# Attention and gated FFN on one Trainium2 core: weight blocks in 2 KB runs, gates ahead of values, and one batch's values rounded elsewhere than on ScalarE

## Chip, cores and metric

One core of a Trainium2 chip (trn2). The metric is device time in microseconds (us) of one execution. An execution of this kernel takes some 2 us longer than the span that its profile shows.

## The reference

```python
q, k, v: [8, 8, 576, 64]            # batch, heads, sequence, head_dim, fp32
kv  = einsum('bhsd,bhse->bhde', k, v)
o   = einsum('bhsd,bhde->bhse', q, kv)
a   = o / sqrt(mean(o*o, -1) + 1e-6) * g_norm
x   = a.transpose(0, 2, 1, 3).reshape(4608, 512)
xn  = x / sqrt(mean(x*x, -1) + 1e-6) * rms_g
out = (silu(xn @ w_gate) * (xn @ w_val)) @ w_out    # w_gate, w_val: 512 x 1536; w_out: 1536 x 512
```

## The kernel before

The kernel works batch by batch: up-projections (gate and value) and down-projection of one batch on TensorE, with the attention of the next batch threaded between them. All matrix work is in bf16; everything arrives in fp32, is staged in one of seven buffers, and is rounded into its bf16 place by VectorE, ScalarE or GpSimd. The rounding of gate and value weights also multiplies the rows by the norm's scale. The order on each engine is written by hand. Batch 0 is the start-up: its first half runs while the first weights come in, and the remaining weights come in during its second half.

Gate and value weights are 1536 columns wide and come in five column blocks; the first four are 256 columns wide, which is 1 KB of fp32 per row, 512 KB per block:

```python
W_BLOCKS = [(0, 2), (2, 4), (4, 6), (6, 8), (8, 12)]      # in units of 128 columns
def load_w(blk, name, queue):
    ...
    queue.dma_start(out=ap, in_={"g": wg_view, "v": wv_view}[name][:, :, j0 * 128 : j1 * 128])
# ...
for blk in range(2):                  # order of the transfers: g0, v0, g1, v1, then g2, v2, g3, v3, g4, v4
    for name in ("g", "v"):
        load_w(blk, name, nc.sync)
```

The first products of batch 0 come in that order too: gate 0, value 0, rows of the attention output, gate 1, two transposes, value 1. TensorE then goes on to the second half of the rows. Loads, the stores of the output and the transposing transfers that turn the queries all share the sync queue, in the order written:

```python
ffn.down_out(2)                       # down_out(1), above, issued two output stores; the next line issues two more
ffn.down_out(3)
cast_q(2, slice(4, 8), DVE)
# ...
for c in range(T):
    atts[2].q_rows(c)                 # four transposing transfers of batch 2's queries
# ... in the loop over batches, n == 1 (the up-projection of batch 1):
steps[0] += [lambda i=i: cast_kv(2, "v", i, SC) for i in (0, 1)]     # batch 2's values, on ScalarE
steps[1] += [lambda i=i: cast_kv(2, "v", i, SC) for i in (2, 3)]
steps[0] += [lambda name=name: cast_kv(2, name, NS, GP) for name in ("k", "v")]
```

ScalarE also does the silu of each gate product, in the order written: a silu stands behind the casts ahead of it. A product lies in a bank of PSUM (TensorE's output memory), which TensorE writes again only when the silu has read it.

## Time and profile before

| | us |
|---|---|
| median of the first three runs | 321.17 (320.72 to 321.30) |
| the run that the profile shows | 322.3, span 320.4 |
| before first gate product | 17.39 |
| first gate product to batch 1's up-projection | 39.10 |
| batch 1's first gate product to batch 2's key-value products | 7.83 |
| from there to the next gate product | 3.16 |
| from there to the last matmul | 248.83 |

In the lines PE is TensorE (PEld its weight loads), ACT ScalarE, DVE VectorE, POOL GpSimd and SPq the sync queue. A timeline line is: start, duration, engine, source line, operation, output and inputs, shapes, the number of instructions put together, and in brackets the idle time ahead of it with what ended it. Neither the duration nor the bracket is to be trusted for a stall: matmuls overlap, so the step from one start to the next is what counts.

### The profile page before, as it was taken

What the parts mean: (1) busy time and instruction counts of PE and PEld (TensorE: products, weight loads), DVE (VectorE), ACT (ScalarE), POOL (GpSimd) and SP (SyncE); (2) the same over time, 40 slices, a digit from 0 to 9 for tenths busy, and PEclk for the clock granted to TensorE, in tenths of its full rate; (3) what the DMA queues carried; (4) which work ended last, traced back from release to release, by engine and by line L of the source; (5) the groups of instructions that cost most, each with busy time, mean ns of one, the idle gap of its engine ahead of it and who ended that gap; (6) DMA issues with size and microseconds to landing.
All of it is one profiled execution on the core that took longest, in us unless ns stands there. A gap on an engine that the chain in (4) does not pass through costs nothing.

```text
span 320.4 us, 5591 instructions
## 1 busy us (share of the span) xinstructions
PE 309.1 (96%) x2138; PEld 151.1 (47%) x2175; DVE 181.5 (57%) x371; ACT 178.9 (56%) x318; POOL 21.0 (7%) x44
## 2 busy tenths in 40 slices
PE   7799999999999999999999999999999999999995
PEld 3475456454444444444444444444544444444443
DVE  4676857479528932794179517950696069604310
ACT  3576457675768376837673767467644374233321
POOL 1153442100000000000000000000000000000000
PEclk9999999999999999999999999999999999999998
DMA  7999999988299747943793379946002610240014
GB/s 255 348 349 387 380 374 305 232 248 211 49 150 315 179 103 190 288 110 75 198 316 103 66 183 215 319 103 190 13 0 51 172 43 1 50 149 0 1 35 98
DMA packets 74440, 54.90 MB, mean 171 GB/s; under 512 B 42281, under 2 KB 67117, under 8 KB 74413
## 3 DMA queue, kind: packets, MB, share of 16 engines
q1 hardware_dynamic: 74044, 53.89, 60.7%
q10 hardware_dynamic: 368, 0.66, 0.6%
q8 instruction: 17, 0.28, 0.3%
q14 instruction: 11, 0.08, 0.1%
HBM read 37.75 MB, written 9.44 MB: 147 GB/s over the span
## 4 chain that ended last, share of the span: by engine, by line
PE 78%; DMA 14%; DVE 2%; SPq 2%; issue 1%; another core or an unknown queue 1%; ACT 1%; POOL 0%; ACTq 0%; DVEq 0%
PE g_ps L490 26%; PE v_ps L490 25%; PE o_ps L532 22%; DMA st<-in_moe_w_out_dram 7%; DMA st<-in_moe_w_val_dram 3%; DMA st<-in_v_dram 2%; PE att_ps L275 1%; DMA st<-in_k_dram 1%; SPq L194 1%; DMA xnt<-xna 1%; DVE xna L394 1%; DMA out_dram<-o_sb 1%; PE att_ps L354 1%; SPq L401 1%
## 5 line engine op out<-in xcount | busy, mean ns | idle before, releaser
L496 DVE TENSOR_TENSOR h_sb<-silu,v_ps 128x512 bf16<-128x512 bf16 x104 | 71.0, 684 | 100.1 <-ACT silu L495 72.4
L490 PE MATMUL v_ps<-xnt,wv_sb 128*128 128x512 bf16 x409 | 106.1, 379 | 0.6
L490 PE MATMUL g_ps<-xnt,wg_sb 128*128 128x512 bf16 x398 | 104.6, 379 | 1.6 <-ACT silu L495 0.7
L495 ACT ACTIVATE silu<-g_ps 128x512 bf16<-128x512 f32 x104 | 61.9, 596 | 67.9 <-PE g_ps L490 52.7
L532 PE MATMUL o_ps<-wo_sb,h_sb 128*128 128x512 bf16 x386 | 87.1, 379 | 0.5
L490 PEld LDWEIGHTS <-wv_sb 128*128 128x128 bf16 x416 | 40.6, 98 | 49.2 <-DVE wv_sb L204 0.5
L532 PEld LDWEIGHTS <-h_sb 128*128 128x128 bf16 x420 | 40.7, 98 | 47.9 <-issue 0.3
L490 PEld LDWEIGHTS <-wg_sb 128*128 128x128 bf16 x416 | 39.5, 98 | 47.7 <-issue 1.6
L106 ACT COPY o_sb<-o_ps 128x512 f32<-128x512 f32 (+1 forms) x34 | 19.7, 581 | 38.0 <-PE o_ps L532 35.3
L106 ACT CAST vb<-st 128x512 bf16<-128x512 f32 (+2 forms) x34 | 19.5, 626 | 6.9 <-DMA st<-in_v_dram 6.9
L394 DVE TENSOR_TENSOR xna<-outa,s1y 128x512 bf16<-128x512 bf16 x28 | 17.9, 685 | 0.0
L377 DVE TENSOR_REDUCE ssq<-sqt 128x16 f32<-128x1024 bf16 x14 | 17.1, 1220 | 0.5
L377 DVE TENSOR_REDUCE ssq<-sq 128x16 f32<-128x1024 bf16 x14 | 17.1, 1220 | 0.5
L106 ACT CAST qb<-st 128x1024 bf16<-128x1024 f32 (+1 forms) x17 | 15.4, 943 | 2.4 <-DMA st<-in_q_dram 2.2
L106 ACT CAST kb<-st 128x512 bf16<-128x512 f32 (+1 forms) x25 | 14.0, 619 | 0.0
L363 ACT ACTIVATE sq<-att_ps 128x512 bf16<-128x512 f32 x14 | 7.6, 594 | 4.3 <-PE att_ps L354 3.6
L376 DVE TENSOR_TENSOR sq<-sq,gsq 128x512 bf16<-128x512 bf16 x14 | 5.9, 422 | 4.9 <-ACT sq L363 4.9
L633 PE MATMUL att_ps<-kv_all 128*128 128x512 bf16 (+1 forms) x21 | 7.3, 471 | 1.2 <-DVE sel L622 1.2
L108 POOL CAST wo_sb<-st 128x512 bf16<-128x512 f32 x12 | 7.5, 657 | 7.3 <-DMA st<-in_moe_w_out_dram 7.3
L363 ACT ACTIVATE sqt<-o_ps 128x512 bf16<-128x512 f32 x14 | 7.6, 597 | 0.0
L368 ACT CAST outa<-att_ps 128x512 bf16<-128x512 f32 x14 | 7.5, 592 | 0.0
L368 ACT CAST outa<-o_ps 128x512 bf16<-128x512 f32 x14 | 7.5, 592 | 0.0
(145 smaller groups left out, 179.8 us busy)
## 6 DMA issues: line engine op xcount, KB each, us to landing
out_dram<-o_sb SPq DMA_DIRECT2D x14, 512.0 KB, 3.0
st<-in_q_dram SPq DMA_DIRECT2D x6, 1024.0 KB, 7.2
st<-in_k_dram SPq DMA_DIRECT2D x6, 1024.0 KB, 10.3
st<-in_v_dram SPq DMA_DIRECT2D x6, 1024.0 KB, 11.2
st<-in_moe_w_out_dram SPq DMA_DIRECT2D x6, 512.0 KB, 11.5
st<-in_moe_w_gate_dram SPq DMA_DIRECT2D x4, 512.0 KB, 10.0
st<-in_moe_w_val_dram SPq DMA_DIRECT2D x4, 512.0 KB, 10.4
st<-in_k_dram SPq DMA_DIRECT2D x4, 288.0 KB, 4.8
```

What stands on the lines that cost most here:

```text
L106: engine.copy(out=dst, in_=src)
L108: engine.tensor_copy(out=dst, in_=src)
L363: SC.activation(out=self.sq[i][:, :, 0, g:H:2, :], in_=self.banks[i][g], func=ACT.Square)
L368: SC.copy(out=rows[:, :, g:H:2, :], in_=self.banks[i][g])
L376: DVE.tensor_tensor(out=sq[:, 1], in0=sq[:, 0], in1=gsq8, op=OP.mult)
L377: DVE.reduce_sum(out=self.ssq[:, c], in_=sq, axis=AX.X)
L394: DVE.tensor_tensor(out=self.xna[c], in0=self.outa[c], in1=self.alpha[:, c, :].to_broadcast([128, H, D]), op=OP.mult)
L490: PE.matmul(ps, lhsT=wt[:, s, j * 128 : (j + 1) * 128], rhs=x[:, s, :], start=(s == 0), stop=(s == NS - 1),)
L495: SC.activation(out=silu, in_=g_ps, func=ACT.Silu)
L496: DVE.tensor_tensor(out=self.h[:, j, :], in0=silu, in1=v_ps, op=OP.mult)
L532: PE.matmul(self.o_ps[c], lhsT=self.h[:, j, c * 128 : (c + 1) * 128], rhs=wo_sb[:, j, :], start=(j == 0), stop=(j == NF - 1),)
L633: PE.matmul(ps[:, 0:w], lhsT=warm_sb[:, 0:128], rhs=warm_sb[:, 0:w], start=True, stop=True, skip_group_check=True)
```

## The change

Its intent: weight blocks two to a buffer in 2 KB runs (the first two gate blocks stay in 1 KB runs), so that transfers go faster; the two first gate blocks ahead of the value blocks, so that TensorE does not wait for gate 1; the value blocks by halves of the rows; the two small vectors issued from ScalarE's queue; and batch 2's values off ScalarE, so that silu does not stand behind a load.

```diff
-    def load_w(blk, name, queue):
-        j0, j1 = W_BLOCKS[blk]
...
+    def load_w(name, blks, split):
...
+            if split:
+                w_st[name, b] = whole[:, :, at : at + w]
+            else:
+                w_st[name, b] = flat[:, NS * at : NS * (at + w)].rearrange("p (s f) -> p s f", s=NS)
+                nc.sync.dma_start(out=w_st[name, b], in_=view[:, :, j0 + at : j0 + at + w])
...
+        if split:
+            for s in (0, 2):
+                nc.sync.dma_start(out=whole[:, s : s + 2], in_=view[:, s : s + 2, j0 : j0 + at])
...
-    load_q0(0, nc.sync)
-    nc.sync.dma_start(out=gam[0:NS, :], in_=moe_rms_g.rearrange("(s p) -> s p", p=128))
+    nc.scalar.dma_start(out=gam[0:NS, :], in_=moe_rms_g.rearrange("(s p) -> s p", p=128))
... (the same for g_norm)
+    load_q0(0, nc.sync)
...
-    for blk in range(2):
-        for name in ("g", "v"):
-            load_w(blk, name, nc.sync)
+    load_w("g", (0, 1), False)
+    load_w("v", (0, 1), True)
...
+    for blk, s in ((0, 0), (0, 1), (1, 0), (0, 2), (1, 1), (1, 2)):
+        round_w(blk, "v", s, GP)
... (products in the order gate 0, rows, gate 1, value 0, transposes, value 1)
-    for blk in (2, 3, 4):
-        for name in ("g", "v"):
-            load_w(blk, name, nc.sync)
+    for name in ("g", "v"):
+        load_w(name, (2, 3), True)
+    for name in ("g", "v"):
+        load_w(name, (4,), False)
... (GpSimd's roundings of blocks 2 and 3: gates first)
-            steps[0] += [lambda i=i: cast_kv(2, "v", i, SC) for i in (0, 1)]
-            steps[1] += [lambda i=i: cast_kv(2, "v", i, SC) for i in (2, 3)]
-            steps[0] += [lambda name=name: cast_kv(2, name, NS, GP) for name in ("k", "v")]
+            steps[0] += [lambda: cast_kv(2, "k", NS, GP)]
+            steps[0] += [lambda i=i: cast_kv(2, "v", i, GP) for i in (0, 1, NS)]
+            steps[2] += [lambda i=i: cast_kv(2, "v", i, DVE) for i in (2, 3)]
```

## The prediction

> **What bounds the kernel now.** First the busy shares and the forty slices of the page, for the bound.
>
> ```profile
> PE 309.1 (96%) x2138; PEld 151.1 (47%) x2175; DVE 181.5 (57%) x371; ACT 178.9 (56%) x318; POOL 21.0 (7%) x44
> ...
> PE   7799999999999999999999999999999999999995
> ...
> DMA  7999999988299747943793379946002610240014
> ```
>
> TensorE is busy in every slice but the first two and the last; the transfers fill only the first eight slices (64 us). Each slice is 8 us. So the change, which touches loads and roundings of the first 65 us, can pay only where TensorE stands still in that stretch. As busy time hides gaps and overlaps, I read TensorE's timeline by start times: four 512-column matmuls advance 0.86 us (59.08 to 59.94), two groups of eight 128-column ones 0.87 us, eight 256-column ones 0.87 us (22.57 to 23.45). What advances more than that is a stall.
>
> The timeline of TensorE, 17 to 23 us, where the first weights come in:
>
> ```profile
> 18.08 0.61 PE L507 MATMUL g_ps<-xnt,wg_sb 128*128 128x128 bf16 x8
> 18.53 1.04 PE L507 MATMUL v_ps<-xnt,wv_sb 128*128 128x256 bf16 x8
> 19.40 0.61 PE L443 MATMUL o_ps<-kv_all,qt 128*128 128x128 bf16 x8
> 20.02 0.28 PE L507 MATMUL g_ps<-xnt,wg_sb 128*128 128x256 bf16 x1
> 20.48 0.94 PE L507 MATMUL g_ps<-xnt,wg_sb 128*128 128x256 bf16 x7 [0.17 <-POOL wg_sb L204]
> 21.25 0.61 PE L288 MATMUL att_ps<-identity,xna 128*128 128x128 bf16 x8
> ```
>
> Between 19.40 and 21.25 lie 0.45 + 0.87 us of work in 1.85 us: a stall of 0.5 us, waiting for the second gate block's roundings.
>
> GpSimd's timeline tells when the blocks landed, by the waits that a transfer ended:
>
> ```profile
> 19.33 1.09 POOL L204 TENSOR_SCALAR wg_sb<-st,rowscale 128x256 bf16<-128x256 f32 x2 [1.41 <-DMA st<-in_moe_w_gate_dram]
> ...
> 23.83 0.48 POOL L204 TENSOR_SCALAR wv_sb<-st,rowscale 128x256 bf16<-128x256 f32 x1 [1.02 <-DMA st<-in_moe_w_val_dram]
> ...
> 26.83 0.48 POOL L204 TENSOR_SCALAR wv_sb<-st,rowscale 128x256 bf16<-128x256 f32 x1 [1.02 <-DMA st<-in_moe_w_val_dram]
> ...
> 32.22 1.36 POOL L204 TENSOR_SCALAR wv_sb<-st,rowscale 128x512 bf16<-128x512 f32 x2 [3.97 <-DMA st<-in_moe_w_val_dram]
> ```
>
> Blocks of 512 KB in 1 KB runs: two in the 3.00 us from 23.83 to 26.83, so 1.50 us each. The two 1 MB blocks in 2 KB runs: 5.39 us to 32.22, so 2.70 us per MB against 3.00. The table of stretches says the same of the rate:
>
> ```profile
> 14.00:24.00 10.00, 9.57 (x114) 7.65 (x115) 7.46 (x22) 7.41 (x16) 5.70 (x13) 1.00 1.10 350
> 26.00:36.00 10.00, 9.84 (x48) 4.41 (x47) 6.91 (x13) 5.98 (x11) 2.78 (x5) 1.00 1.05 388
> ```
>
> The last number is GB/s: 350 with 1 KB runs, 388 with runs of 2 KB and more, with the engines full (share over 1) both times.
>
> Last, ScalarE and then TensorE at the start of batch 1's up-projection:
>
> ```profile
> 57.62 0.64 ACT L495 ACTIVATE silu<-g_ps 128x512 bf16<-128x512 f32 x1
> 60.82 1.14 ACT L106 CAST vb<-st 128x512 bf16<-128x512 f32 x2 [2.56 <-DMA st<-in_v_dram]
> 61.86 0.59 ACT L495 ACTIVATE silu<-g_ps 128x512 bf16<-128x512 f32 x1
> ```
>
> ```profile
> 60.80 1.03 PE L490 MATMUL v_ps<-xnt,wv_sb 128*128 128x512 bf16 x4
> 62.50 1.02 PE L490 MATMUL g_ps<-xnt,wg_sb 128*128 128x512 bf16 x4 [0.67 <-ACT silu L495]
> ```
>
> ScalarE's in-order stream stands 2.56 us behind batch 2's values; the second silu comes late, its PSUM bank is not free, and TensorE steps 1.70 us where 0.86 is due: 0.84 us lost. It is the largest single stall of TensorE after 17 us. A small one stands at 46.01, where four matmuls take 1.09 instead of 0.86: 0.2 us until the second down-weight block, landed at about 45.2, is rounded.
>
> **What the Trainium skill says.** "DMA: Bandwidth & Descriptors", § Why small descriptors are slow (HBM only): each packet carries about 3 cycles beside one per 32 bytes. As an estimate from that page, 1 KB runs cost 35 cycles and 2 KB 67, so two short ones are 4% dearer than a long one; this trace shows 3.00 against 2.70 us, 11%, and I use the trace. The same page, § Issuing engines are not separate DMA queues: issuing from another engine saves only sequencer time. The trace agrees: issuing the two small vectors holds the sync queue 0.55 and 0.70 us. "SBUF — State Buffer", § Who interferes with whom: a GpSimd instruction and a VectorE one that takes the shared ports block each other. That bears on moving casts to GpSimd: its 128x512 casts took 0.59 us each in the pairs of 1.18 us, 0.70 in those that met a busy VectorE (1.40 and 1.44).
>
> **The change, part by part.**
>
> *Small vectors to ScalarE's queue.* It frees 1.25 us of the sync queue (3.14 to 4.44), but the next issue, at 4.49, follows the first key block's landing (its cast starts at 4.47), and the compiled order lists a wait on that transfer there, in both kernels. So the third key block is issued no earlier, and the transfers are full by then. Worth 0 to 0.1 us; I count 0.
>
> *2 KB runs.* The first value MB and the MBs of gate and value of blocks 2 and 3 gain 0.30 us each, so all that comes later lands about 0.9 us sooner. TensorE gets only the 0.2 us at 46.01 of this. The rest lands in slack.
>
> *Gates before values, values by halves of the rows.* Order now: gate 0, gate 1, upper rows of values 0+1, lower rows. Four pieces of 512 KB as before, so the second piece lands in time for the second gate block, whose roundings end about 18.3 instead of 20.9. The 0.5 us stall goes. TensorE, starting as before at 17.39, does gate 0 and sums (to 18.53), rows (0.45), gate 1 (0.87) and is at value 0 at 19.85. But the third piece lands at 19.25 less 0.15 = 19.1, the fourth 1.35 later, 20.45. GpSimd rounds six pieces at 0.47 each: (0,0) 19.57, (0,1) 20.04, (1,0) 20.5, (0,2) 20.97, (1,1) 21.4, (1,2) 21.9, while ScalarE does (0,3) and (1,3) from 20.45, to 21.4. Value 0's third row block is there at 21.0. TensorE then needs two matmuls of the first unit and four of the second: 0.65, so 21.65; the two transposes 0.45, to 22.1; value 1 0.87, to 22.97. Before, this point was 22.57: +0.40. I chose to let the waits stand wholly on the path: the fixed order on TensorE has nothing to put there.
>
> *ScalarE's table load* slips from 21.29 to 21.4, the first silu from 22.58 to about 22.7; its bank is next needed about 24.7. Free.
>
> *Later roundings.* Blocks 2 and 3 now round gates before values on GpSimd. The value half needed at about 27.6 lands near 25.9 (20.45 + 4 x 1.35), its first two roundings end at 26.8. No new stall.
>
> *Batch 2's values.* Four ScalarE casts (1.14 + 1.12 us) become two on GpSimd, two on VectorE. The values land about 59.8 instead of 60.8; GpSimd does two casts and the tail at 0.6 to 0.7, to about 61.8; VectorE does its two in 0.75 after the third product, to about 63.4; TensorE wants them from 63.6 on. The silu no longer waits: -0.84.
>
> Sum: +0.40 - 0.20 - 0.84 = -0.64 us, which 321.17 turns into 320.5. From batch 2 on nothing differs but the start, so the shift is carried to the end.
>
> **The rivals.**
> 1. *The value wait grows.* Should the third piece land late, or GpSimd be blocked by VectorE (0.70 for 0.47 on six pieces), value 0 waits another 0.5 to 0.8 us. For it: the chain third piece, four roundings, TensorE has no slack. Time 321.0 to 321.3.
> 2. *The value wait is short.* If the roundings run nearer the landings, or the start moves up 0.2 us with the freed sync queue, the reorder costs nothing: 319.9 to 320.1. Against it: the wait on the first transfer.
> 3. *The gain at 62 us turns into another wait.* The key-value products follow 1.7 us later, and the rotated queries of batch 2 come by transposing transfers landing near 66.4, when TensorE, 0.64 us sooner, reaches them at about 66.3. Losing half of the 0.84 gives 320.9. In favour: those issues follow the output stores, which follow TensorE at 55 us, not the removed stall. Against: only the last quarter of the products needs the last transpose.
> 4. *The loads bound everything*, as the chain of waits suggests with its 14% for transfers. Then 0.9 us more would come off: 319.6. Against it: TensorE's timeline has no such waits between 27 and 60 us other than the 0.2.
>
> **Range and chances.** The measured runs of before span 0.6 us, and the rivals lie between 319.6 and 321.3. I predict 320.5, with 319.7 to 321.4 holding it 8 times in 10. Two per cent would be 6.4 us, ten times my sum; the stalls of the whole touched stretch do not add up to 2 us. So: faster 0.005, same 0.985, slower 0.01.
>
> **What would show it.** Right: in the new timeline of TensorE no step of 1.7 us near 61 us, and no gap before the second gate block, but about 1.1 us of gap within value 0 near 20 us; the stretch 26 to 62 us 0.2 us shorter; GB/s near 385 from about 19 us on; batches from the third on moved as a block by some 0.6 us. Wrong: the first values rounded by 20 us (reorder free), a wait before batch 2's products on GpSimd's casts or on a transpose (rival 3), or later batches whose period of 32.6 us (123.07 to 155.69 in the chain of waits) changes.

## The result, and the profile after

| | median us | lowest to highest | runs |
|---|---|---|---|
| before | 321.41 | 320.72 to 321.96 | 6 |
| after | 321.40 | 320.82 to 322.33 | 6 |

The ratio is 1.0002, with a 95% interval of 0.9981 to 1.0022: the same. (A ratio is the mean time of one kernel's fast runs over that of the other's of the same rounds, so not quite the ratio of the medians.) I had predicted 320.5; what was measured is 0.9 us above that, at the very edge of the range. The class was right, the gain was not there.

The page of the changed kernel. TensorE's busy time is what it was, and the transfers fill the same slices.

```profile
span 319.0 us, 5591 instructions
...
PE 308.9 (97%) x2138; PEld 151.3 (47%) x2175; DVE 181.4 (57%) x372; ACT 176.6 (55%) x313; POOL 22.8 (7%) x48
...
PE   7899999999999999999999999999999999999995
...
DMA  7999999888389757924792499946002600230014
```

This span is 1.4 us shorter than the one of before, and that is the trap: the profiled run of before took 322.3 us, that of after 321.24. The two traces differ by about 1.1 us, the two kernels by nothing.

The table of stretches (busy time of PE, PEld, DVE, ACT, POOL; granted clock, DMA share, GB/s) shows that the 2 KB runs do what they were meant to, 385 GB/s where there were 350:

```profile
14.00:24.00 10.00, 9.51 (x111) 7.74 (x110) 8.19 (x22) 7.54 (x15) 7.48 (x16) 1.00 1.05 385
26.00:36.00 10.00, 10.00 (x48) 4.51 (x46) 7.03 (x15) 6.00 (x10) 2.81 (x5) 1.00 1.05 387
```

GpSimd's timeline tells the landings. The first values had landed by 17.84; the last rows of blocks 2 and 3 (24.45) and block 4 (29.90) landed 2.3 to 2.4 us sooner than in the trace of before (26.83, 32.22):

```profile
14.66 2.74 POOL L207 TENSOR_SCALAR wg_sb<-st,rowscale 128x256 bf16<-128x256 f32 x6 [0.87 <-DMA st<-in_moe_w_gate_dram]
17.84 2.74 POOL L207 TENSOR_SCALAR wv_sb<-st,rowscale 128x256 bf16<-128x256 f32 x6 [0.44 <-DMA st<-in_moe_w_val_dram]
21.74 1.99 POOL L207 TENSOR_SCALAR wg_sb<-st,rowscale 128x256 bf16<-128x256 f32 x4 [1.15 <-DMA st<-in_moe_w_gate_dram]
24.45 1.84 POOL L207 TENSOR_SCALAR wv_sb<-st,rowscale 128x256 bf16<-128x256 f32 x4 [0.72 <-DMA st<-in_moe_w_val_dram]
29.90 1.36 POOL L207 TENSOR_SCALAR wv_sb<-st,rowscale 128x512 bf16<-128x512 f32 x2 [3.62 <-DMA st<-in_moe_w_val_dram]
```

TensorE's timeline over the first weights. Gate 1 (18.23) now follows without a gap, and value 0 waits within itself, after its second matmul: it takes 1.30 us to the transposes (19.10 to 20.40) where 0.87 is due. So the wait is 0.43 us by the steps (the bracket says 0.25), where I had expected about 1.1; my own sums gave 0.93 (19.85 to 21.65 for 0.87 of work).

```profile
18.23 1.04 PE L510 MATMUL g_ps<-xnt,wg_sb 128*128 128x256 bf16 x8
19.10 0.38 PE L510 MATMUL v_ps<-xnt,wv_sb 128*128 128x256 bf16 x2
19.73 0.83 PE L510 MATMUL v_ps<-xnt,wv_sb 128*128 128x256 bf16 x6 [0.25 <-POOL wv_sb L207]
20.40 0.61 PE L291 MATMUL att_ps<-identity,xna 128*128 128x128 bf16 x8
...
21.72 1.04 PE L510 MATMUL o_ps<-xnt,wg_sb 128*128 128x256 bf16 x8
```

Then ScalarE and TensorE at 60 us. No cast stands between the silus, and gate follows value in 0.86 us (59.94 to 60.80). But after the key-value products there is a new wait, on the transposed queries:

```profile
58.47 0.60 ACT L498 ACTIVATE silu<-g_ps 128x512 bf16<-128x512 f32 x1 [1.08 <-PE g_ps L493]
60.20 0.60 ACT L498 ACTIVATE silu<-g_ps 128x512 bf16<-128x512 f32 x1 [1.13 <-PE g_ps L493]
```

```profile
59.94 1.03 PE L493 MATMUL v_ps<-xnt,wv_sb 128*128 128x512 bf16 x4
60.80 1.03 PE L493 MATMUL g_ps<-xnt,wg_sb 128*128 128x512 bf16 x4
61.66 1.03 PE L493 MATMUL v_ps<-xnt,wv_sb 128*128 128x512 bf16 x4
62.62 0.82 PE L278 MATMUL att_ps<-vb,kb 128*64 128x64 bf16 x40
...
66.09 0.29 PE L357 MATMUL o_ps<-kv_all,qt 64*128 64x64 bf16 x8 [0.36 <-DMA qt<-qb]
66.31 0.60 PE L493 MATMUL g_ps<-xnt,wg_sb 128*128 128x512 bf16 x2
```

From the key-value products (62.62) to the next gate product (66.31) TensorE took 3.69 us; before, it had been 3.16 (64.32 to 67.48). The queue's own timeline shows why the queries are late: the four transposing issues take 6.0 us and stand behind the four output stores.

```profile
55.00 3.70 SPq L555 DMA_DIRECT2D out_dram<-o_sb  x4
58.81 6.01 SPq L319 DMA_TRANSPOSE qt<-qb  x4
```

So the profile shows the stall that I wanted away gone (7.83 to 7.00 us), 0.53 us of it spent again on another wait, and times that do not differ. What remained to be found out was whether the 0.84 us had been there to gain at all.

### The profile page after: what moved, and what is told of

Same layout as the page of the kernel before. It is cut to its first block, busy times and chain, and to the rows that moved or that the text cites. A ratio compares the mean times of both kernels' runs of the same rounds, so it can differ in the third digit from the quotient of the medians.

```text
span 319.0 us, 5591 instructions
## 1 busy us (share of the span) xinstructions
PE 308.9 (97%) x2138; PEld 151.3 (47%) x2175; DVE 181.4 (57%) x372; ACT 176.6 (55%) x313; POOL 22.8 (7%) x48
## 4 chain that ended last, share of the span: by engine, by line
PE 87%; DMA 6%; SPq 2%; issue 1%; DVE 1%; another core or an unknown queue 1%; ACT 1%; POOL 1%
PE v_ps L493 27%; PE g_ps L493 27%; PE o_ps L535 26%; DMA st<-in_moe_w_val_dram 3%; DMA st<-in_q_dram 2%; PE att_ps L278 1%; SPq L319 1%; DMA qt<-qb 1%; PE v_ps L535 1%; PE g_ps L535 1%; DMA out_dram<-o_sb 1%; POOL wv_sb L207 1%; PE o_ps L510 1%; PE att_ps L357 1%
## 5 line engine op out<-in xcount | busy, mean ns | idle before, releaser
L106 ACT CAST vb<-st 128x512 bf16<-128x512 f32 (+2 forms) x30 | 17.2, 628 | 3.3 <-DMA st<-in_v_dram 3.3
```

Source lines behind the costliest of these rows:

```text
L106: engine.copy(out=dst, in_=src)
```

## The experiments

All kernels gave correct results and ran in five timed rounds. A job of four kernels shares eleven runs of the kernel before on the same chip. The theory going in, called S: the stall at 62 us is the difference of two times (when batch 2's values land, and when TensorE wants the PSUM bank behind ScalarE's casts), so its size is a property of one run. The rivals: the gain is real and given back in the wait for the queries; the new order of the first blocks eats it; the loads bound everything.

### First job: both kernels again, and the values alone

`before_again` and `after_again` are the two kernels unchanged.

> The kernel before, unchanged, for a second trace and for the noise. Theory N (the 0.75 us by which the changed kernel reached the first gate matmul sooner, 16.64 against 17.39 us, is chance in the first loads): this trace reaches that matmul at some other time, 16.4 to 17.2, its span is 319.0 to 320.0, and the stalls (0.5 us before the second gate block, 0.84 us at 62 us) are there again. Theory V (the moved small vectors made the head start): it is at 17.3 to 17.5 again. Time ratio 1.000 within 0.0015.

> The changed kernel, unchanged. Theory N: the first gate matmul anywhere from 16.4 to 17.4 us; the time ratio to before 0.998 to 1.000, as what is gained after that matmul is about 0.4 us in its first trace (0.84 at 62 us and 0.1 before, less 0.53 at the batch 2 products). Theory V: matmul at 16.5 to 16.8 again and ratio about 0.996 (1.2 us).

| | median us | lowest to highest | ratio to before (95%) |
|---|---|---|---|
| before of this job, 11 runs | 321.42 | 320.49 to 323.37 | |
| before_again | 321.13 | 320.76 to 321.78 | 0.9993 (0.9969 to 1.0017) |
| after_again | 321.38 | 320.84 to 321.99 | 0.9995 (0.9969 to 1.0022) |

The second trace of the very same kernel is the most telling one. ScalarE and TensorE in it:

```profile
59.56 1.14 ACT L106 CAST vb<-st 128x512 bf16<-128x512 f32 x2 [1.86 <-DMA st<-in_v_dram]
60.61 0.59 ACT L495 ACTIVATE silu<-g_ps 128x512 bf16<-128x512 f32 x1
```

```profile
60.25 1.03 PE L490 MATMUL v_ps<-xnt,wv_sb 128*128 128x512 bf16 x4
61.25 1.02 PE L490 MATMUL g_ps<-xnt,wg_sb 128*128 128x512 bf16 x4
```

The casts start at 59.56 instead of 60.82, and the stall is 1.00 - 0.86 = 0.14 us instead of 0.84. The size of the "largest single stall" of my prediction belonged to one run, in which the load trailed: of the 16 signals that the trace holds for that load, 14 had come by 59.38, the last two at 60.32 and 60.80; in this trace all had come by 59.54. This gives a rule that can be checked: the casts and the silu put the next gate product 1.69 us after the start of the casts (60.82 to 62.50 in the first trace, 59.56 to 61.25 in this one), or 0.86 us after the value product ahead of it, whichever is later.

`values_only` is the kernel before with the last hunk of the diff alone; `values_undone` is the changed kernel without that hunk.

> Before, with batch 2's values rounded off ScalarE and nothing else. If that is the whole source of the gain after 22 us: no 0.84 us stall at 62 us, and 0.3 to 0.6 us of it lost again where the batch 2 products wait for the transposed queries, ratio 0.9985 to 0.9995 (0.15 to 0.5 us). Rival (the gain is kept whole when the loads are not sooner): no wait at the products, ratio 0.9974 (0.84 us).

> The changed kernel, with batch 2's values on ScalarE again. Values land near 58.5 us there, so if ScalarE's wait for the values made the stall, the second silu is held until about 59.7 rather than 61.9 and the stall at the fourth gate product is small, 0 to 0.3 us, even with the casts on ScalarE: then the sooner loads, not the move, would be enough. Rival: the stall is back with 0.5 us or more. Ratio to before 0.998 to 1.001.

| | median us | lowest to highest | ratio to before (95%) |
|---|---|---|---|
| values_only | 321.25 | 320.58 to 322.55 | 0.9999 (0.9972 to 1.0026) |
| values_undone | 321.48 | 320.61 to 322.69 | 1.0002 (0.9973 to 1.0032) |

In `values_only` the stall is gone (7.00 us to the key-value products), the wait for the queries that I had expected did not show (3.16 us to the next gate product: a miss), and the time does not move. GpSimd's first cast of the values starts at 60.27 there; by the rule, casts on ScalarE would have put the gate product at about 61.9, where TensorE did it at 61.16. So the move spared this trace an estimated 0.7 to 0.8 us, which six runs with an interval of ± 0.9 us cannot show. `values_undone` tells more. Its casts are on ScalarE as before:

```profile
58.86 1.14 ACT L106 CAST vb<-st 128x512 bf16<-128x512 f32 x2 [1.10 <-DMA st<-in_v_dram]
59.90 0.59 ACT L498 ACTIVATE silu<-g_ps 128x512 bf16<-128x512 f32 x1
```

58.86 + 1.69 is 60.55, and TensorE comes to that product at 61.17: no stall, though its first gate product (17.38) was as late as in the first trace of before (17.39). In this trace the sooner loads alone are enough to end the stall; the move of the casts then has nothing left to do. The other eight traces with the long runs of blocks 2 and 3 (`late_after`, below, aside) agree: GpSimd's first cast of the values starts between 57.89 and 59.11, and 1.69 us later is in each at least 0.2 us before TensorE did the gate product. In the traces with short runs (`late_before` and the faulty `runs_1kb`, below, aside) it is the other way: 0.11 to 0.84 us of stall in the four with casts on ScalarE, and an estimated 0.7 to 0.8 in `values_only` and in `runs_1kb_mended`, below (60.08 against 60.95).

### Second job: values made late, the order undone, the short runs

`late_before` and `late_after` add two loads of 256 KB, never read, ahead of batch 2's values, into unused ends of the staging buffers:

```diff
         for name in ("k", "v"):
             alloc_kv(b, name)
+            if b == 2 and name == "v":
+                for i in (-1, -2):
+                    load_spare(i, 3)      # 128 rows x 8 heads of batch 3's keys, in 256-byte runs
             load_kv(b, name, nc.sync)
```

> Before, with two loads of 256 KB in short runs, never read, queued ahead of batch 2's values. Theory S (ScalarE's wait for the values is the stall, and its size is only how late the values land: landing + 1.05 us of casts + 0.6 us of silu, less the time when TensorE wants the bank; 0.8 us in the first trace, 0.14 in the second, where they landed 1.3 us sooner): the values land 2.6 to 3.8 us later, near 62.1 to 63.3, and TensorE stands 2.5 to 3.8 us there; ratio 1.007 to 1.012. Rival (the stall has another cause): 0.1 to 0.8 us as before, ratio 1.000 to 1.002.

> The changed kernel with the same two loads. Theory S: the silus go on, TensorE waits only later, at batch 2's key-value products, for GpSimd's third cast (the tail), about 2 us after the landing: 1.0 to 1.8 us, ratio 1.003 to 1.005; so the move is worth 1.5 to 2 us where the values are late, and nothing where they are in time. Rival: the late landing costs both kernels the same, ratio as late_before within 0.001.

| | median us | lowest to highest | ratio to before (95%) |
|---|---|---|---|
| before of this job, 11 runs | 321.69 | 321.12 to 322.30 | |
| late_before | 322.92 | 322.42 to 324.71 | 1.0039 (1.0017 to 1.0061) |
| late_after | 321.94 | 321.11 to 322.49 | 1.0003 (0.9988 to 1.0018) |

With late values the whole change is worth 1.0039 - 1.0003, about 0.36% or 1.2 us. In `late_before` I had expected twice that; its profiled run, at 324.71 us, was its slowest, and the others left no trace. In `late_after` I had expected 1.003 to 1.005 and a wait of 1.0 to 1.8 us for GpSimd's casts, and neither came. Lines of TensorE's waits (total, times, longest), one of each kernel, late_before first:

```profile
PE g_ps L504 <- ACT silu L509: 2.3, 1, 2.3
```

```profile
PE o_ps L371 <- DMA qt<-qb: 1.0, 1, 1.0
```

In the one the silu is waited for, in the other not, and there the queries are waited for instead. So the mechanism of the prediction is shown, and so is its rival. But the 1.2 us are not the worth of the move alone, as the long runs land the values sooner in `late_after`, late as they are (ScalarE's casts in `late_before`, then GpSimd's in `late_after`):

```profile
62.09 1.14 ACT L106 CAST vb<-st 128x512 bf16<-128x512 f32 x2 [4.17 <-DMA st<-in_v_dram]
```

```profile
60.20 1.73 POOL L108 CAST vb<-st 128x512 bf16<-128x512 f32 x3 [4.23 <-DMA st<-in_v_dram]
```

By the rule, casts on ScalarE would have cost `late_after` an estimated 0.9 us (60.20 + 1.69 is 61.89, and TensorE did that product at 60.99), and its wait for the queries, 1.14 us by the steps (4.30 for 3.16), is longer than that. What the move alone is worth with late values was not run. From the up-projection's start to the key-value products `late_before` took 11.02 us, 4.0 more than 7.00, of which the wait is 2.45 by the steps (60.46 to 63.77 for 0.86; the bracket says 2.3). The rule holds here too (casts at 62.09, gate product at 63.77). The other 1.6 us are the clock (columns as in the stretches above; the last but two is the granted clock):

```profile
60.00:64.00 4.00, 1.72 (x8) 0.68 (x7) 0.25 (x1) 1.91 (x4) 0.61 (x1) 0.99 1.21 342
64.00:68.00 4.00, 4.00 (x49) 1.70 (x48) 1.78 (x3) 1.84 (x4) 0.00 (x0) 0.58 0.71 115
```

After the gap the granted clock was 0.58 in this stretch, and two groups of four matmuls stepped 1.55 and 1.85 us, where 0.86 and 0.96 are usual. The Trainium skill, "TensorE: Matmul & The Clock Gate", § Part 1: The HAM clock gate (the "warmup" mystery), tells of such a gate: half rate after an idle window of about 3.4 us. The trace agrees on the half rate (its record of the clock holds 0.5 for 3.41 us, from 63.91 on), but here an idle gap of 2.3 us came before it.

`order_undone` loads blocks 0 and 1 and orders their roundings and products as the kernel before does (1 KB runs, g0 v0 g1 v1), and leaves the other parts of the change in. `runs_1kb` was meant to undo the 2 KB runs alone:

```diff
-    load_w("v", (0, 1), True)
+    load_w("v", (0, 1), False)
...
-        load_w(name, (2, 3), True)
+        load_w(name, (2, 3), False)
```

> The changed kernel with loads, roundings and products of blocks 0 and 1 in the old order (gate 0, value 0, gate 1, value 1 in 1 KB runs), the rest as changed. My prediction's term (new order costs 0.40 us): from the first gate matmul to the second half's first product about 0.4 us less than the mean of the new order's traces (5.08, 5.49, 4.84: 5.14), so 4.7 to 4.8, ratio 0.999. Theory N (both orders wait for a load whose landing moves from run to run against the first gate matmul): anywhere from 4.8 to 5.3, as the old order gave 5.18, 5.11 and 4.97; ratio 0.999 to 1.001.

> The changed kernel with blocks 0 to 3 in 1 KB runs, block by block, gates of 0 and 1 still ahead of values. If shorter runs cost 0.30 us per MB: 1.50 us between landings instead of 1.35 up to block 3, the fifth megabyte block lands about 0.9 us later than in the changed kernel at equal start, and as all of that is slack the ratio is 0.999 to 1.001. Rival (the loads bound the stretch to 60 us): 0.6 to 0.9 us longer, ratio 1.002 to 1.003.

| | median us | lowest to highest | ratio to before (95%) |
|---|---|---|---|
| order_undone | 320.98 | 320.14 to 322.26 | 0.9979 (0.9960 to 0.9998) |
| runs_1kb | 321.99 | 321.65 to 322.52 | 1.0008 (0.9994 to 1.0022) |

`runs_1kb` was a faulty experiment. GpSimd's order of roundings was left as it is for halves of the rows, where the first row block of value 1 comes ahead of the third of value 0. With whole blocks this makes value 0 wait for the landing of value 1. GpSimd:

```profile
18.54 0.94 POOL L207 TENSOR_SCALAR wv_sb<-st,rowscale 128x256 bf16<-128x256 f32 x2 [0.68 <-DMA st<-in_moe_w_val_dram]
20.05 1.85 POOL L207 TENSOR_SCALAR wv_sb<-st,rowscale 128x256 bf16<-128x256 f32 x4 [0.57 <-DMA st<-in_moe_w_val_dram]
```

TensorE waited 1.2 us there by the bracket (1.5 by the steps). So the run tells nothing of short runs, and was mended in the last job.

### Third job: the vectors, the order again, the transposes first

`vectors_only` is the kernel before with the two small vectors issued from ScalarE's queue ahead of the first query load; `vectors_undone` is the changed kernel with them back on the sync queue, behind it. `order_undone_again` is a repeat. `turns_first` is `order_undone` with the four transposes issued ahead of the last two output stores:

```diff
     ffn.down_out(2)
-    ffn.down_out(3)
     cast_q(2, slice(4, 8), DVE)
+    att2 = Att(2)
+    for c in range(T):
+        att2.q_rows(c)
+    ffn.down_out(3)
```

> Before, with the two small vectors on ScalarE's queue and nothing else. First gate matmul so far: 17.39, 16.81, 17.12, 17.18 us with them on the sync queue; 16.64, 17.29, 17.38, 16.42, 16.15, 16.61 with them moved. Theory N (chance): 16.2 to 17.4, third key block issued at about 4.5 again, ratio 0.999 to 1.001. Theory V (the move gains about 0.4 us on average): 16.1 to 16.9, ratio 0.998 to 0.9995.

> The changed kernel with the two small vectors on the sync queue again. Theory N: first gate matmul anywhere from 16.2 to 17.4, ratio to before 0.999 to 1.001. Theory V: 16.9 to 17.4, and slower than the changed kernel by about 0.4 us, ratio 1.0005 to 1.002.

> The changed kernel with blocks 0 and 1 in the old order, once more, as its first ratio (0.9979, 0.9960 to 0.9998) is the only one clear of 1. If the old order is truly better than the new one by about 0.5 us: ratio 0.997 to 0.999 again. If it was chance: 0.999 to 1.001.

> As order_undone, and the four transposing transfers of batch 2's queries issued ahead of the second pair of output stores. They wait for the query casts alone, so they start near 56.2 us rather than 58.8 and the last lands near 63 us: no wait at batch 2's products (it was 0.25 to 0.96 us in four traces), from the key-value products to the next gate product 3.15 to 3.2 us instead of 3.3 to 4.3. Ratio 0.997 to 0.9985. Rival (the wait only moves, to the third batch's loads behind the late stores): 3.2 us there, but the gain lost later and ratio as order_undone.

| | median us | lowest to highest | ratio to before (95%) |
|---|---|---|---|
| before of this job, 11 runs | 321.20 | 320.70 to 322.32 | |
| vectors_only | 320.97 | 320.43 to 321.51 | 0.9987 (0.9971 to 1.0004) |
| vectors_undone | 321.12 | 320.89 to 321.69 | 0.9996 (0.9981 to 1.0011) |
| order_undone_again | 321.26 | 320.60 to 323.56 | 0.9999 (0.9978 to 1.0020) |
| turns_first | 320.67 | 320.36 to 321.08 | 0.9979 (0.9963 to 0.9995) |

The gain of `order_undone` was not repeated; from the first gate product to the second half its traces took 5.37 and 4.89 us, within the 4.84 to 5.49 of the new order's. One of the runs of the repeat, at 323.56 us, is the profiled one, and shows what such an outlier can be. A line of TensorE's timeline and three stretches of it:

```profile
11.31 0.69 PE L276 MATMUL att_ps<-vb,kb 64*64 64x64 bf16 x18 [1.96 <-ACT vb L106]
```

```profile
8.00:12.00 4.00, 1.96 (x30) 1.38 (x30) 1.75 (x5) 1.37 (x3) 0.00 (x0) 0.88 1.02 356
12.00:16.00 4.00, 4.00 (x44) 2.40 (x44) 1.94 (x10) 1.76 (x4) 1.36 (x3) 0.50 1.09 355
16.00:20.00 4.00, 3.73 (x32) 2.60 (x31) 2.47 (x8) 2.14 (x5) 3.37 (x8) 0.77 1.07 372
```

Batch 0's values were late, TensorE stood 1.96 us, and then ran at half clock from 11 to 18 us; its first gate product was at 19.83. The wait of 2 us made some 3 us of loss. The other slow runs left no trace, but their granted clock is on record. Of the 119 runs of the four jobs that enter the fit below, 17 have a mean clock of 0.995 or less; they took 322.37 us in the mean, the other 102 took 321.16, and all four above 322.6 us are among the 17 (323.37 of before at 0.993, 323.17 of `turns_before` at 0.994, this one at 0.989). So a spell at half clock goes with the slow end of the scatter; what began it in those runs is not known.

`vectors_only` shows the rule of 1.69 us at work once more: the casts start at 59.28, the gate product at 60.97.

### Fourth job: transposes first in both kernels, and the short runs mended

The first two add the move of the transposes alone to the changed kernel and to the kernel before; the third repeats `turns_first`; the fourth is `runs_1kb` with GpSimd's order put right, value block 0 whole ahead of block 1, and blocks 2 and 3 loaded as g2 v2 g3 v3 as before:

```diff
-    for blk, s in ((0, 0), (0, 1), (1, 0), (0, 2), (1, 1), (1, 2)):
+    for blk, s in ((0, 0), (0, 1), (0, 2), (1, 0), (1, 1), (1, 2)):
```

> The changed kernel with one thing more: the four transposing transfers of batch 2's queries are issued ahead of the last two output stores of batch 0, not behind all four. Theory (what is gained before 62 us is partly given back in the wait for these transposes): the wait, 0.36 and 0.21 us in the two traces of the changed kernel, is gone, the step from the key-value products to the next gate products is 3.16 us, and the time falls by that much, 0.2 to 0.4 us: ratio 0.9985 to 0.9995 to the kernel before. Rival (the wait costs nothing, or the loads issued behind the stores pay for it): the ratio stays at 0.9995 to 1.0005, or a wait on batch 3's loads appears near 80 us.

> The kernel before with that move of the transposes alone. Theory: its traces show no wait for the transposes above 0.1 us, as the stall for the silu or a later start comes first, so nothing is to be had: ratio 0.9995 to 1.0005, and the stall near 62 us, 0.1 to 0.9 us by the landing of batch 2's values, stands. Rival (the early transposes are worth 0.2% of themselves, which is what the kernel with the order undone seemed to say): 0.998.

> A repeat of the kernel with the order of the first blocks undone and the transposes first, which gave 0.9979 (0.9963 to 0.9995). If that was the kernel's own: 0.997 to 0.999 again and a step of 3.16 us to the next gate products. If it was chance of the job's runs, as the first 0.9979 of the order undone seems to have been: 0.999 to 1.000.

> The changed kernel with the first four weight blocks loaded block by block in runs of 1 KB, the first two gate blocks still ahead of the value blocks, and GpSimd's roundings in the order in which blocks land (the earlier kernel of this kind kept an order made for halves of the rows, so that value block 0 waited for value block 1). Theory (the longer runs land the later loads some 0.9 us sooner, but that is slack but for about 0.2 us): the wait ahead of value block 0 is again 0 to 0.7 us, from the first gate product to the second half's first product 4.8 to 5.5 us, pieces land 1.50 us apart, ratio 0.9995 to 1.001. Rival (loads bound the first 60 us): 0.9 us more, ratio 1.002 to 1.003.

| | median us | lowest to highest | ratio to before (95%) |
|---|---|---|---|
| before of this job, 11 runs | 321.54 | 320.70 to 322.52 | |
| turns_after | 321.37 | 321.01 to 321.58 | 0.9991 (0.9974 to 1.0008) |
| turns_before | 321.21 | 320.75 to 323.17 | 0.9996 (0.9970 to 1.0021) |
| turns_first_again | 320.65 | 320.05 to 321.59 | 0.9971 (0.9952 to 0.9990) |
| runs_1kb_mended | 321.08 | 320.61 to 321.81 | 0.9984 (0.9965 to 1.0002) |

In `turns_after` the wait for the queries is gone. Its sync queue and TensorE:

```profile
55.38 1.23 SPq L555 DMA_DIRECT2D out_dram<-o_sb  x2
56.93 5.63 SPq L319 DMA_TRANSPOSE qt<-qb  x4
62.67 1.19 SPq L555 DMA_DIRECT2D out_dram<-o_sb  x2
```

```profile
65.83 0.40 PE L357 MATMUL o_ps<-kv_all,qt 64*128 64x64 bf16 x16
66.16 1.04 PE L493 MATMUL g_ps<-xnt,wg_sb 128*128 128x512 bf16 x4
```

The step is 3.16 us (63.00 to 66.16), and the ratio lies where the theory put it, though its interval includes 1. `turns_before` has nothing to gain from it and gains nothing; its stall is 0.11 us, and the rule hits it again (casts at 60.03, gate product at 61.72). `runs_1kb_mended` is not slower than the changed kernel: value 0 follows gate 1 almost without a wait (0.96 us for 0.87), presumably because its third row block is GpSimd's third rounding there and not its fourth (4.94 us from the first gate product to the second half, against 5.08 and 5.49), and the later, slower blocks find slack. The repeat of `turns_first` came out as the first time, with the same median within 0.02 us: it beats the kernel before by 0.2 to 0.3%, which is still "the same" at 2%. The changed kernel was not run beside it as it is.

The stages of the traces, from TensorE's start times (us):

| trace | first gate product | to second half | to batch 1 | to key-value products | to next gate product | to last matmul | run |
|---|---|---|---|---|---|---|---|
| before | 17.39 | 5.18 | 33.92 | 7.83 | 3.16 | 248.83 | 322.30 |
| before_again | 16.81 | 5.11 | 34.01 | 7.13 | 3.28 | 248.67 | 321.03 |
| turns_before | 16.69 | 5.79 | 33.95 | 7.11 | 3.16 | 248.61 | 321.32 |
| after | 16.64 | 5.08 | 33.90 | 7.00 | 3.69 | 248.56 | 321.24 |
| after_again | 17.29 | 5.49 | 33.98 | 7.00 | 3.37 | 248.48 | 321.96 |
| turns_after | 17.00 | 5.05 | 33.95 | 7.00 | 3.16 | 248.48 | 321.06 |
| turns_first | 16.37 | 4.94 | 34.16 | 7.00 | 3.16 | 248.62 | 320.36 |
| turns_first_again | 16.62 | 4.97 | 34.16 | 7.00 | 3.16 | 248.52 | 320.53 |
| runs_1kb_mended | 16.86 | 4.94 | 33.97 | 7.00 | 3.16 | 248.55 | 320.83 |

Last, all timed runs of these kernels together, without `late_before`, `late_after` and `runs_1kb`: 131 runs, fitted by least squares with one level for each job and one amount for each part of the change. One run scatters by 0.62 us about the fit. The amounts, with one standard error:

| part | predicted us | fitted us |
|---|---|---|
| vectors on ScalarE's queue | 0 | -0.19 ± 0.15 |
| new order with halves of the rows | +0.40, and -0.20 for the 2 KB runs | +0.16 ± 0.16 |
| batch 2's values off ScalarE | -0.84 | -0.10 ± 0.15 |
| transposes ahead of two stores (not in the change) | | -0.25 ± 0.19 |

The three parts of the change add up to -0.13 us, which is nothing against their errors. The long runs of blocks 2 and 3 stayed in when the order was undone, so they have no row of their own. Without the 17 runs at a clock of 0.995 or less (and without the first result's 12, of which half have no clock on record) one run scatters by 0.42 us, and the same fit gives -0.25 ± 0.11, +0.38 ± 0.12, -0.21 ± 0.12 and -0.11 ± 0.14, in the order of the table; the first three add up to -0.07 ± 0.11. To choose runs by their clock is to choose by something that the change may itself alter, so this is a hint and no more: the new order may cost what was predicted for it, and the other parts pay it back.

## Why the prediction was wrong, point by point

**Batch 2's values off ScalarE: the term that was mis-sized.** I put -0.84 us. The move itself does what it was meant to: in `values_only` the stall is gone, and with values made late the silu no longer stands behind the casts. But before had a stall of 0.84 us in one trace only; the other traces with its casts and its loads show 0.14, 0.11 and, with the vectors moved, 0.37. With the short runs the stall is anything from 0.1 to 0.84 us, by when the values land. The fit over all runs gives -0.10 ± 0.15. The step that failed is therefore the reading "1.70 where 0.86 is due: 0.84 us lost" as a property of the kernel. My own text had a second warning: it let the values land a microsecond sooner through the 2 KB runs. With the 1.69 us rule, casts at 59.8 give a gate product at 61.5 where 61.66 is due. By my own numbers the stall was gone before the casts moved, so two parts of the change cured the same stall, and `values_undone` and the landings in eight more traces show that the sooner loads are enough.

**Rival 3, the wait for the queries: undervalued.** I gave it half of the 0.84 us and kept it out of the sum. It happened: 0.53 and 0.21 us of wait by the steps in the two traces of the changed kernel, 3.69 and 3.37 instead of 3.16 us. In `turns_after` it is gone (it is absent from `runs_1kb_mended` too, so it comes and goes with the run). TensorE reached the queries 1.69 us sooner (65.21 for 66.90), and the sync queue issued the transposes only 0.74 sooner (58.81 for 59.55), much as the rival said.

**The order of gates and values, +0.40: not seen in the traces.** The stretch from the first gate product to the second half took 4.84 to 5.49 us in six traces with the new order (5.1 in the mean), and 4.89 to 5.79 in ten with the old one (5.2). The reorder moves the wait from gate 1 to value 0, and either wait is as long as the landing makes it: by the steps 0.43 us in `after`, 0.84 in `after_again`, none in `values_undone`. Timings allow a loss: +0.16 ± 0.16, or +0.38 ± 0.12 without the runs at a low clock. I had added up six roundings at 0.47 us behind a third landing at 19.1; that landing was by 17.84, of which 0.75 us is the sooner start of that run.

**The 2 KB runs, -0.20: the rate was right, the gain was not.** 512 KB land 1.35 us apart (21.74 to 24.45 for two of them), as estimated, and not 1.50. The wait at 46 us that I counted on was replaced: TensorE's transposes of the queries ahead of it took 1.19 us instead of 1.06, and then 0.95 instead of 1.09, so 2.14 instead of 2.15 together. In that trace GpSimd's roundings of the down weights now met VectorE's query cast, which took 0.56 us instead of 0.43; that this is the cause was not tested. `runs_1kb_mended`, without the long runs, is not slower than the changed kernel.

**The vectors, 0:** open. They may be worth 0.2 us (-0.19 ± 0.15; `vectors_only` 0.9987 with an interval that just includes 1).

**Later batches, no change:** right. From the next gate product to the last matmul the traces take 248.5 to 248.8 us.

**The range:** I took it from a spread of 0.6 us over three runs of before. Eleven runs spread over 1.2 to 2.9 us. A sum of -0.64 us was the size of one run's scatter, and the profiled run was itself 0.9 us above the median of the six; of the 1.1 us by which the two profiled runs differ, 0.75 lay ahead of the first gate product (17.39 against 16.64), where the kernels hardly differ.

What stays open: why `turns_first`, with the old order of the first blocks, is faster than `turns_after`, with the new one, by 0.6 us in the means of one job. The traces do not tie it to the order: the former's first gate product comes 0.4 to 0.6 us sooner, which the first loads scatter by anyway, the stretch after it is 0.1 us shorter, and the one before batch 1 is 0.2 us longer. The fit without the low-clock runs points at the order (+0.38 ± 0.12), without showing the place.

## What to carry to other kernels

A stall behind a load is the difference of two times, and each scatters from run to run: before a stall is counted as gain, look at it in a second trace, and check whether the profiled run is a typical one. When two parts of a change end the same stall, count it once, and ask what stands next in line just behind it; here it was a transpose queued behind stores, and a swap in the queue's order fixed it. When the parts of a change are each smaller than the scatter of a run, only many runs with parts taken in and out can size them.

## What the Trainium skill lacked or had wrong

- "TensorE: Matmul & The Clock Gate", § HAM oscillation — how this bites in real kernels: it advises no idle gaps of TensorE above about 3.4 us. Here gaps of 1.96 and 2.3 us were followed by half the clock, for 6.83 and 3.41 us (two and one times the page's window), and one of 1.47 us at the same place (11.03 in before) was not; the wait of 2.3 us cost 4.0 in all.
- "DMA: Bandwidth & Descriptors", § Why small descriptors are slow (HBM only): its count of cycles per packet, taken alone, makes two runs of 1 KB 4% dearer than one of 2 KB, as an estimate; measured were 1.50 against 1.35 us for 512 KB, 11%. The page also names the descriptor's own bytes, without a cost for them.
- "Runtime: NRT & Kernel Launch", § Instruction fetch mechanics: it calls the cost of crossing a 16 KiB boundary of the instructions mostly hidden, and says nothing of the other transfers. In the traces such a packet of 16,384 bytes holds one of the 16 DMA engines for 1.1 us (at 17.03 us in before, at 15.56 and 25.24 in after), among the loads of the weights. That it delays a landing is likely and was not tested.
- No page that I read says how far runs of one program scatter: 0.62 us about the fit here, 320.5 to 323.4 us over eleven runs of one kernel, so that one trace can be 0.9 us off the median; nor that a spell at half clock marks the slow end (322.37 against 321.16 us in the mean).
